# A state-space mixer times a spatial-shift MLP: new norms, polar form, layouts and a written-out instruction order

## The chip, the cores and the metric

The kernel runs on one core of one Trainium2 chip. Its time is the device time of one launch in microseconds, the median of several runs. A core has five engines that run side by side, each with its own queue in fixed order: TensorE (PE, matrix multiplication), VectorE (DVE, element-wise), ScalarE (ACT, table functions and copies), GpSimd (POOL, hardly used here) and SyncE (SP, which issues the DMAs). They wait for each other through semaphores.

## The reference

The input `u` is 2048 steps by 512 channels. It is normalised, and two branches work on the result; their product is added to the input.

```python
xn = _layernorm(x, axis=-1)
s = _A_ref(xn, A_re, A_im, B_re, B_im, C_re, C_im, log_dt, Dskip)
g = _silu(_B_ref(xn, w1, w2, w3, w4))
return x + s * g
```

Branch A is a long convolution. Its kernel `K[d, l]` is the real part of the sum over 128 states of `C * exp(dt * A * l) * dt * B`, complex; the convolution is done by FFT, and `xn * Dskip` is added. Branch B works along the steps and channels:

```python
h = _gelu(_layernorm(x) @ w1)
# the four quarters of h are shifted by +1, -1, +2, -2 steps
x1 = x + shifted(h) @ w2
return x1 + _gelu(_layernorm(x1) @ w3) @ w4
```

with `w1`, `w2` 512 x 512, `w3` 512 x 1376 and `w4` 1376 x 512.

## The kernel before

The 2048 steps are kept as 16 tiles of 128 partitions by 512 channels, one array `X`. Tile `s` holds the steps that are `s` modulo 16, with the four blocks of partitions in the order 0, 2, 1, 3 (`ORDER`). A shift by one or two steps is therefore mostly another tile; only at the two ends (tiles 0, 1 and 14, 15) does a shift also move by one partition. `wrapped` builds these shifted rows as copies into a tile `hw`.

The stages, by function:

- `loads` brings in X, the weights and the coefficients; `params` turns the coefficients into logarithm, angle, phase and magnitude for each channel and state. The phase and magnitude of `B * C` come from a polar form: the smaller over the larger of the two absolute values, an arctangent, and corrections for the swap and for both signs.
- `token_mixing` is branch B up to `x1`: `ln_first` normalises X (the first and the second norm in one step), `h_pair` transposes two tiles and multiplies by `w1` (f32, tile `pb`), `hs_pair` multiplies the shifted tiles by `w2` (f32, tile `pd`), `ln_second` prepares the norm for the MLP. `rstd` is an inverse square root by a guess and three Newton steps of three instructions on DVE. `u_stage1` makes the first stage of the FFT of u, stored in DRAM (`scr_Ud`); `weight_squares` and `prep` scale `w3` and `w4` and split them into f16 halves.
- `u_spectra` computes u's spectra of one half of the channels and stores them (`scr_Uh`).
- `tables(0)` and `tables(1)` compute the convolution kernel of one half of the channels each, in 8 tiles of 32 channels. `block` makes magnitudes (`mag`, `EB`) by exponentials on ACT; `phases`, `remainders`, `waves` and `sums` make sines and cosines and the products on DVE (`pt`), and two groups of 64 matmuls (`pc<-pt`) sum over the states.
- `kstage1` and `products` are the FFT stages: spectra, complex products, and the way back (`pr`, `z1e`), through DRAM.
- `mlp` multiplies by `w3` (`pb<-x1T,w3h`, 12 matmuls of one group, f16 in three passes), applies gelu and multiplies by `w4` (`pa<-w4h,ghl`, 6 matmuls of one group), for 8 groups of two tiles.
- `gate`, `inverse` and `finish` apply silu, multiply by the convolution's result and add the input.

None of this is issued in the order of the code. Each call is recorded as an operation of a `Plan`, with its cost in a model and its dependencies; a group in `together` is one operation. Operations of `E` (`Either`) can go to ACT or to DVE, the final stores to SP or ACT. `Plan.order` then schedules the list: whenever an engine is free it takes, of the ready operations, the one with the smallest due time (`DUE`, one number for each operation), with added prices for a change of ACT's table (`SWITCH`), of TensorE's mode (`KEEP`) and for the choice between ACT and DVE (`PREFER`, `AVOID` and their PSUM forms). `Plan.issue` emits the instructions in that order, with a table load wherever ACT's set changes and with warm-up matmuls (`fill`) where the model sees TensorE waiting. All instructions carry line 515 in the profile (512 for table loads, 514 for warm-up matmuls).

Of the kernel before, what the change touches and what calls it, by code (L numbers as in the profile page):

```python
# [10 lines left out]
F32 = mybir.dt.float32  # L11
# [8 lines left out]
P = 128  # L20
# [7 lines left out]
TWO_PI = 6.283185  # L28
INV_2PI = float(np.float32(1.0 / (2.0 * np.pi)))
# [63 lines left out]
class Op:  # L93
    __slots__ = (
        "eng", "alts", "calls", "cost", "deps", "succ", "table", "vt", "idx", "nbytes", "n", "ready", "start",
        "alias", "first", "last", "psum", "mode", "stage", "dma", "room", "fresh", "free_at", "fill",
# [23 lines left out]
SHIFT, KEEP = 0.09, 1.0  # L120
FETCH = 1.3, 5.0, 2.5
WORDS, ASKED, HELD, MORE = 256, 150, 449, 1.0065
WARM = 36
QUARTERS, EIGHTHS, SPECTRUM = 1.78, 1.8, 0.93
UP, DOWN = 1.31, 1.297

DUE = (
# [129 lines left out]
)  # L257
SWITCH = 20.74
PREFERP, AVOIDP = 12.42, -13.86
PREFER, AVOID = -0.38, -5.84  # L260

# [1266 lines left out]
```

## Time and profile before

| | |
|---|---|
| median of 3 runs | 562.91 us (561.33 to 565.46) |
| the profiled execution | 561.96 us, span in the profile 560.2 us |
| PE busy | 533.4 us, 95% |
| DVE busy | 466.1 us, 83% |
| ACT busy | 410.2 us, 73% |
| ACT table loads | 49, 62.9 us |
| DMA | 103.14 MB, 184 GB/s |

The span runs from the first to the last instruction of one execution. "Busy" of an engine counts the time in which at least one of its instructions runs; consecutive instructions overlap a little. Matmuls are pipelined, so PE's busy share is not its share of peak. Groups of instructions are listed as engine, operation, output tile <- input tiles, shapes and count, then busy time and mean duration in ns of one, then the engine's idle time before them with what ended it. The chain of work that ended last lists start, duration and what ran. The table of stretches lists for each engine the busy time and the number of instructions, then the granted TensorE clock, the DMA share and GB/s.

### The profile page before, as it was taken

To read this page: it belongs to the slowest core of one execution; us is meant where nothing else is said; L and a number is where in the kernel's file an instruction comes from. 1 tells how busy PE (TensorE), PEld (TensorE's weight loads), DVE (VectorE), ACT (ScalarE), POOL (GpSimd) and SP (SyncE) were. 2 spreads that over 40 slices of the span, in tenths; PEclk is the share of its full clock that TensorE was granted. 3 is DMA by queue.
4 is the path that set the end of the run, shared out by engine and by line. 5 is a ranking of instruction groups with operands and counts; after the bars stand their busy time and mean duration, and the time that the engine had idled before them with its cause. 6 is when DMAs were issued, how large, how long until landed. Compare 5 with 4: busy or idle time off the path is not lost.

```text
span 560.2 us, 14282 instructions
## 1 busy us (share of the span) xinstructions
PE 533.4 (95%) x6104; PEld 349.6 (62%) x6104; DVE 466.1 (83%) x710; ACT 410.2 (73%) x588; POOL 0.7 (0%) x6
## 2 busy tenths in 40 slices
PE   7989999989899899999999999999999999999982
PEld 7967677855344466656766666676676665675630
DVE  5999999999999998999999999999415168564276
ACT  2999997999987998998899999768246235224420
POOL 0000000000000000000000000000000000000000
PEclk9999999999999899999999999999999999999995
DMA  9975667535647252735333431453886669859947
GB/s 205 229 214 190 233 222 253 180 117 165 196 143 263 96 140 68 217 140 186 112 100 100 133 131 60 142 162 124 264 281 236 225 190 281 254 156 277 327 130 223
DMA packets 69695, 103.14 MB, mean 184 GB/s; under 512 B 14784, under 2 KB 48832, under 8 KB 68736
## 3 DMA queue, kind: packets, MB, share of 16 engines
q1 hardware_dynamic: 68864, 100.13, 57.8%
q10 hardware_dynamic: 768, 2.10, 1.2%
q8 instruction: 48, 0.79, 0.6%
q14 instruction: 15, 0.12, 0.1%
HBM read 64.46 MB, written 37.75 MB: 182 GB/s over the span
## 4 chain that ended last, share of the span: by engine, by line
PE 72%; DVE 15%; ACT 5%; DMA 5%; issue 2%; SPq 1%; DVEq 0%; ACTq 0%
PE pb L515 29%; PE pa L515 21%; PE pd L515 11%; PE pc L515 11%; DVE pt L515 9%; DVE X L515 3%; DMA X<-in_A_u_dram 2%; ACT mag L515 2%; DMA w<-in_B_w_dram 2%; ACT pt L515 1%; DVE w4h L515 1%; SPq L515 1%; ACT L512 1%; DVE w3h L515 1%; DMA out_dram<-X 0%
## 5 line engine op out<-in xcount | busy, mean ns | idle before, releaser
L515 PE MATMUL pb<-x1T,w3h 128*128 128x256 f16 (+1 forms) x1056 | 123.4, 273 | 2.7 <-issue 1.2
L515 PE MATMUL pa<-w4h,ghl 128*128 128x512 f16 (+1 forms) x528 | 121.7, 379 | 0.0
L515 PEld LDWEIGHTS <-w3h 128*128 128x128 f16 (+1 forms) x1056 | 102.6, 100 | 28.5 <-issue 13.9
L515 PEld LDWEIGHTS <-ghl 128*128 128x128 f16 (+1 forms) x528 | 49.9, 98 | 59.7 <-issue 7.5
L515 DVE SCALAR_TENSOR_TENSOR ghl<-g,wsc,ghl 128x512 f16<-128x512 f32 (+1 forms) x48 | 33.6, 700 | 41.7 <-ACT ghl L515 41.6
L512 ACT ACT_TABLE_LOAD x49 | 62.9, 1283 | 7.4 <-DMA out_dram<-X 5.8
L515 PE MATMUL pd<-w,hT 128*128 128x512 f32 x116 | 56.8, 633 | 5.3 <-DVE X L515 4.3
L515 PE MATMUL pb<-xT,w 128*128 128x256 f32 x256 | 59.6, 384 | 1.9 <-ACT hT L515 1.4
L515 ACT ACTIVATE pt<-pt 128x2048 f32<-128x2048 f32 x29 | 55.2, 1906 | 7.6 <-DVE pt L515 7.6
L515 DVE TENSOR_TENSOR pt<-mag,pt 128x1024 f32<-128x1024 f32 x48 | 57.5, 1214 | 0.0
L515 ACT ACTIVATE g<-pb,wsc 128x512 f32<-128x512 f32 (+1 forms) x48 | 30.8, 649 | 35.6 <-PE pb L515 33.8
L515 PEld LDWEIGHTS pb<-xT,w 128*128 128x128 f32 x256 | 47.1, 190 | 13.4 <-ACT hT L515 3.6
L515 ACT ACTIVATE ghl<-g,wsc 128x512 f16<-128x512 f32 (+1 forms) x41 | 28.0, 688 | 30.0 <-PE pa L515 29.7
L515 PEld LDWEIGHTS pd<-w,hT 128*128 128x128 f32 x116 | 22.4, 201 | 33.9 <-issue 26.1
L515 ACT ACTIVATE mag<-par 128x128 f32<-128x128 f32 x160 | 41.0, 452 | 0.2
L515 DVE TENSOR_TENSOR pt<-pt 128x2048 f32<-128x2048 f32 x16 | 36.5, 2280 | 0.0
L515 DVE SCALAR_TENSOR_TENSOR pt<-pt 128x2048 f32<-128x2048 f32 x16 | 36.4, 2277 | 0.0
L515 PEld LDWEIGHTS pc<-pt 128*32 128x32 f32 x2048 | 29.5, 110 | 7.9 <-issue 5.8
L515 PE MATMUL pc<-pt 128*32 128x64 f32 x2048 | 32.5, 220 | 0.0
L515 ACT ACTIVATE pt<-pt,halfpi 128x2048 f32<-128x2048 f32 x16 | 32.0, 1998 | 0.1
L515 DVE TENSOR_TENSOR pr<-pd,uin 128x1024 f32<-128x1024 f32 x16 | 18.9, 1218 | 10.9 <-PE pd L515 10.8
L515 ACT ACTIVATE pt<-pt,magic 128x2048 f32<-128x2048 f32 x12 | 24.0, 1996 | 4.6 <-DVE pt L515 4.6
(149 smaller groups left out, 773.8 us busy)
## 6 DMA issues: line engine op xcount, KB each, us to landing
wst<-in_B_w_dram SPq DMA_DIRECT2D x20, 512.0 KB, 4.2
scr_Ud<-ue SPq DMA_DIRECT2D x16, 512.0 KB, 3.2
uin<-scr_Ud SPq DMA_DIRECT2D x32, 256.0 KB, 4.3
cst<-c_gp SPq DMA_DIRECT2D x16, 384.0 KB, 3.7
scr_Uh<-uh SPq DMA_DIRECT2D x8, 512.0 KB, 3.6
scr_Kfa<-k1e SPq DMA_DIRECT2D x8, 512.0 KB, 2.6
kin<-scr_Kfa SPq DMA_DIRECT2D x16, 256.0 KB, 3.2
scr_Zda<-z1e SPq DMA_DIRECT2D x8, 512.0 KB, 4.7
```

The source lines that it names most:

```text
L512: self.engines["ACT"].preload_act_table_set(SETS[table])
L515: ins = [getattr(self.engines[op.eng], name)(*args, **kw).ins for name, args, kw in op.calls]
```

## The change

The instructions change in these places:

- `rstd`: two third-order steps of four instructions in place of three Newton steps of three.
- `params`: the polar form takes the ratio of difference and sum of the absolute values, so that no swap has to be undone; the two signs become factors of plus or minus one half. The phase is scaled when it is copied into `par`.
- `ln_first`: four groups of tiles (2, 2, 4, 8) in place of five; the chain of the first one is a single operation of the plan. `ln_second`: four groups in place of six.
- The shifted rows are written by the gelu itself (`gelus`), in pieces, for the first and last pair; `wrapped` and `hw` are gone.
- `u_spectra` writes the spectra back into the tile of their inputs; the ring of input tiles and that of constants move.
- `block`: the lower half of the magnitudes (`mag[0]`) and `EB` are laid out in whole rows of 128 channels, so that the exponentials write and the squares read them in one piece; DVE then reads them with a step of 512 bytes.
- `Plan.order` no longer chooses: `SEQUENCE` lists all 1660 operations in order, and `CHOICE` names the engine of each of the 284 operations that have two. The order of the DMAs is part of it.

```diff
-        while len(out) < len(ops):
-            t, e = min(
-                (max(free[e], min(o.ready for o in pool)), e) for e, pool in pools.items() if pool
-            )
...
+        for k in SEQUENCE:
+            pick = ops[k]
+            assert pick.n == 0
+            e = pick.eng
+            t = max(free[e], pick.ready)
...
-        for f in (1.0, 1.0, by):
-            V.scalar_tensor_tensor(t, dst, -0.5 * f, dst, op0=ALU.mult, op1=ALU.mult)
+        for f in (0.375, 0.375 * by):
+            c = f ** 0.5
+            V.scalar_tensor_tensor(t, dst, c, dst, op0=ALU.mult, op1=ALU.mult)
             V.tensor_mul(t, t, x)
-            V.scalar_tensor_tensor(dst, t, 1.5 * f, dst, op0=ALU.add, op1=ALU.mult)
+            V.scalar_tensor_tensor(t, t, -10.0 / 3.0 * c, t, op0=ALU.add, op1=ALU.mult)
+            V.scalar_tensor_tensor(dst, t, 5.0 * f, dst, op0=ALU.add, op1=ALU.mult)
...
-        V.tensor_tensor(swap, tb, ta, op=ALU.is_gt)
-        V.tensor_tensor(am, ta, tb, op=ALU.max)
-        V.tensor_tensor(rat, ta, tb, op=ALU.min)
+        V.tensor_add(am, ta, tb)
+        V.tensor_sub(rat, tb, ta)
...
-        V.tensor_mul(am, am, tb)
+        V.scalar_tensor_tensor(am, tb, SQRT_HALF, am, op0=ALU.mult, op1=ALU.mult)
         V.tensor_mul(am, am, dtb)
+        V.tensor_scalar(sx, wr, 0.0, 0.5, op0=ALU.is_ge, op1=ALU.subtract)
+        V.tensor_scalar(wi, wi, 0.0, 0.5, op0=ALU.is_ge, op1=ALU.subtract)
         A.activation(ph, rat, AF.Arctan)
-        V.tensor_scalar(ph, ph, INV_2PI, None, op0=ALU.mult)
-        V.tensor_scalar(ta, ph, -2.0, 0.25, op0=ALU.mult, op1=ALU.add)
-        V.tensor_mul(ta, ta, swap)
-        V.tensor_add(ph, ph, ta)
-        V.tensor_scalar(tb, wr, 0.0, None, op0=ALU.is_lt)
-        V.tensor_scalar(ta, ph, -2.0, 0.5, op0=ALU.mult, op1=ALU.add)
-        V.tensor_mul(ta, ta, tb)
-        V.tensor_add(ph, ph, ta)
-        V.tensor_scalar(tb, wi, 0.0, -2.0, op0=ALU.is_lt, op1=ALU.mult)
-        V.scalar_tensor_tensor(ph, tb, 1.0, ph, op0=ALU.add, op1=ALU.mult)
+        V.scalar_tensor_tensor(ph, ph, -QUARTER, sx, op0=ALU.add, op1=ALU.mult)
+        V.scalar_tensor_tensor(ph, ph, QUARTER, wi, op0=ALU.add, op1=ALU.mult)
...
-        mag = [at(magn + 4 * K4 * h, [P, 8, BQ, 4], F32, "mag") for h in range(2)]
-        ea = EB[:, : 8 * BQ].rearrange("p (q a) -> p q a", a=8)
-        eb = EB[:, 8 * BQ :].rearrange("p (q b) -> p q b", b=4)
+        rows_of = at(magn, [P, 8, 4, BQ], F32, "mag")
+        mag = [rows_of.rearrange("p b c q -> p b q c"), at(magn + 4 * K4, [P, 8, BQ, 4], F32, "mag")]
+        ea = EB[:, : 8 * BQ].rearrange("p (a q) -> p q a", a=8)
+        eb = EB[:, 8 * BQ :].rearrange("p (b q) -> p q b", b=4)
...
-            uh = usr["uh"]([P, 2, 2, DH], F32, "uh")
+            uh = uin.rearrange("p (l a) d -> p l a d", a=2)
...
+    UP_ROW = ((64, 0, 64), (32, 64, 32), (1, 96, 31)), 0
+    DOWN_ROW = ((0, 64, 64), (64, 32, 32), (96, 1, 31)), 127
+
+    def gelus(j, m2, dst, src):
+
+        if 0 < j < S // 2 - 1:
+            A.activation(dst, src, AF.Gelu_apprx_tanh)
+            return
+        k = 1 if j == 0 else 0
+        steps = slice(0, 2) if m2 else slice(1 - k, 2 - k)
+        A.activation(dst[:, 1 - k], src[:, 1 - k], AF.Gelu_apprx_tanh)
+        if not m2:
+            A.activation(dst[:, k, k], src[:, k, k], AF.Gelu_apprx_tanh)
+        pieces, zero = DOWN_ROW if k else UP_ROW
+        for d, o, n in pieces:
+            A.activation(dst[:, k, steps, d : d + n], src[:, k, steps, o : o + n], AF.Gelu_apprx_tanh)
+        V.memset(dst[:, k, steps, zero : zero + 1], 0.0)
...
-            if j in (0, 1, 2, 4, 6):
-                ln_first(slice(2 * j, 2 * j + (2 if j < 2 else 4)))
+            if j in (0, 1, 2, 4):
+                ln_first(slice(2 * j, 2 * j + (2, 2, 4, 0, 8)[j]))
...
-            if k in (0, 1, 6, 7):
+            if k in (0, 7):
                 ln_second(slice(2 * GROUPS[k], 2 * GROUPS[k] + 2))
-            elif k in (3, 5):
-                ln_second(slice(2 * GROUPS[k - 1], 2 * GROUPS[k - 1] + 4))
+            elif k == 2:
+                ln_second(slice(4, 8))
+            elif k == 6:
+                ln_second(slice(8, 16))
```

More of the change, by code (lines that the diff above doesn't have):

```diff
@@ L28 @@
 TWO_PI = 6.283185
+QUARTER = float(np.pi / 4)
+SQRT_HALF = float(np.sqrt(0.5))
 INV_2PI = float(np.float32(1.0 / (2.0 * np.pi)))
@@ L94 @@
     __slots__ = (
-        "eng", "alts", "calls", "cost", "deps", "succ", "table", "vt", "idx", "nbytes", "n", "ready", "start",
-        "alias", "first", "last", "psum", "mode", "stage", "dma", "room", "fresh", "free_at", "fill",
+        "eng", "alts", "calls", "cost", "deps", "succ", "table", "idx", "nbytes", "n", "ready", "start",
+        "alias", "first", "last", "mode", "dma", "room", "fresh", "free_at", "fill",
     )
@@ L119 @@
 ISSUE = 0.45
-SHIFT, KEEP = 0.09, 1.0
+SHIFT = 0.09
 FETCH = 1.3, 5.0, 2.5
@@ L123 @@
 WARM = 36
+CHAIN = 2.3
 QUARTERS, EIGHTHS, SPECTRUM = 1.78, 1.8, 0.93
 UP, DOWN = 1.31, 1.297
-DUE = (
[129 rows of a table removed]
-)
-SWITCH = 20.74
-PREFERP, AVOIDP = 12.42, -13.86
-PREFER, AVOID = -0.38, -5.84
+SEQUENCE = (
[83 rows of a table added]
+)
+CHOICE = (
+    "AAAAADDAAAAAAADADAAADADDADDADADDDADADDDDDDDDDADDADADDDAAADADDAAAAAAAAAAAAAAAAAAAAAAAAAAADDADDAAAADDA"
+    "AAADAAAAAAADAAAAADAAADDAADDDAADDDAAAAAAAAAAAAAAAAAAAAAAAAAAAAAAAADDADAADDAAAAADAAAAAAAAAAADDDDADAAAA"
+    "AAAAAAAADAADDADDAAADDAAADAADADAADAADDAADADADDAAAAAADSSSSSSSSSSSSASSAASSAASSSSASAAASS"
+)
 class Clock:
@@ L356, in new @@
         op = Op()
-        op.alts, op.table, op.dma, op.psum = {}, table, dma, False
+        op.alts, op.table, op.dma = {}, table, dma
         op.deps, op.alias, op.idx = set(), set(), len(self.ops)
-        op.vt = DUE[op.idx]
         op.room, op.fresh, op.mode = set(), True, 0
@@ L366, in add @@
         op = self.group or self.new(table, dma)
-        op.psum = "PSUM" in str(reads[0].space) if reads else False
         if "PE" in alts:
@@ L433, in order @@
                 ops[d].succ.append(op)
-        pools = {e: [] for e in self.engines}
         free = dict.fromkeys(self.engines, 0.0)
-        def release(op):
-            for e in op.alts:
-                pools[e].append(op)
+        choice = iter(CHOICE)
         for op in ops:
-            if op.n == 0:
-                release(op)
-        table, mode, chan, landed, clock, words, out = 0, 0, 0.0, [], Clock(), Fetch(), []
-        while len(out) < len(ops):
-            t, e = min(
-                (max(free[e], min(o.ready for o in pool)), e) for e, pool in pools.items() if pool
-            )
-            pick, score = None, None
-            for o in pools[e]:
-                if o.ready <= t + 0.02:
-                    v = o.vt
-                    if e == "ACT" and o.table and o.table != table:
-                        v += SWITCH
-                    if e == "PE" and o.mode != mode:
-                        v += KEEP
-                    if len(o.alts) > 1:
-                        on = (PREFERP, AVOIDP) if o.psum else (PREFER, AVOID)
-                        v += on[e != "DVE"]
-                    if pick is None or (v, o.idx) < score:
-                        pick, score = o, (v, o.idx)
-            for k in pick.alts:
-                pools[k].remove(pick)
-            pick.eng = e
+            if len(op.alts) > 1:
+                letter = next(choice)
+                op.eng = next(e for e in op.alts if e[0] == letter)
+            else:
+                op.eng = next(iter(op.alts))
+        table, mode, chan, landed, clock, words, out = 0, 0, 0.0, [], Clock(), Fetch(), []
+        for k in SEQUENCE:
[3 more added lines that the diff above has]
+            t = max(free[e], pick.ready)
             pick.cost, pick.calls = pick.alts[e]
@@ L500, in order @@
                     s.free_at = max(s.free_at, after)
-                if s.n == 0:
-                    release(s)
         self.span = max(max(free.values()), chan)
@@ L766 @@
     gtile = Ring(area(2 * K2), K2, 2)
-    hw = at(gtile.o, [P, 6, P], F32, "hw")
     late = place[0]
@@ L799 @@
     usr = dict(
-        uin=Slots([early + 4 * K4, vtile.o]), uh=Slots([vtile.o + K4, wtile.o]), cst=Ring(wtile.o + K4, K1, 2),
+        uin=Slots([early + 4 * K4, vtile.o + K4]), cst=Ring(gtile.o + K2, K1, 2),
     )
@@ L890, in params @@
         sr = at(phA + 2 * K4, [P, 2, 4, NM], F32, "sr")
-        swap, rat = sr[:, 0], sr[:, 1]
-        V.tensor_tensor(swap, tb, ta, op=ALU.is_gt)
-        V.tensor_tensor(am, ta, tb, op=ALU.max)
-        V.tensor_tensor(rat, ta, tb, op=ALU.min)
+        sx, rat = sr[:, 0], sr[:, 1]
+        V.tensor_add(am, ta, tb)
+        V.tensor_sub(rat, tb, ta)
         V.tensor_scalar(ta, am, 1e-37, None, op0=ALU.max)
@@ L918, in params @@
             for h in range(2):
-                E.copy(
-                    par[:, k, h * DH : h * DH + DH].rearrange("p (m r) -> p m r", r=4),
-                    pt[:, h * DH : h * DH + DH].rearrange("p (r m) -> p m r", r=4),
-                )
+                dst = par[:, k, h * DH : h * DH + DH].rearrange("p (m r) -> p m r", r=4)
+                src = pt[:, h * DH : h * DH + DH].rearrange("p (r m) -> p m r", r=4)
+                if k == 2:
+                    E.affine(dst, src, 2.0 / np.pi)
+                else:
+                    E.copy(dst, src)
     lgr, thr, phr, wmr = par[:, 0, :], par[:, 1, :], par[:, 2, :], par[:, 3, :]
@@ L960, in squares @@
             for h in range(2):
-                A.activation(
-                    mag[b // 4][:, 2 * b % 8 + h : 2 * b % 8 + 2 * n : 2, :, 0:4:2],
-                    mag[0][:, b : b + n, :, 2 * h : 2 * h + 2], AF.Square,
-                )
+                src = rows_of[:, b : b + n, 2 * h : 2 * h + 2]
+                if b == 4:
+                    dst, src = mag[1][:, h : 2 * n : 2, :, 0:4:2], src.rearrange("p b c q -> p b q c")
+                else:
+                    dst = rows_of[:, 2 * b + h : 2 * b + 2 * n : 2, 0:4:2]
+                A.activation(dst, src, AF.Square)
         with plan.together(table=TABLES[AF.Exp]):
@@ L1293, in ln_first, with norms @@
             V.bn_aggr(mv[:, s, 0:2], stats[:, s % 8])
-        var, t = mv[:, ss, 1], tn[:, ss, 0]
-        V.tensor_scalar(t, var, EPS, None, op0=ALU.add)
-        V.reciprocal(t, t)
-        V.tensor_mul(mv[:, ss, 2], var, t)
-        rstd(r12[:, ss], mv[:, ss, 1:3], xe[:, ss], tn[:, ss])
-        V.scalar_tensor_tensor(bs[:, ss], mv[:, ss, 0], -1.0, r12[:, ss, 0], op0=ALU.mult, op1=ALU.mult)
+        def norms():
+            var, t = mv[:, ss, 1], tn[:, ss, 0]
+            V.tensor_scalar(t, var, EPS, None, op0=ALU.add)
+            V.reciprocal(t, t)
+            V.tensor_mul(mv[:, ss, 2], var, t)
+            rstd(r12[:, ss], mv[:, ss, 1:3], xe[:, ss], tn[:, ss])
+            V.scalar_tensor_tensor(bs[:, ss], mv[:, ss, 0], -1.0, r12[:, ss, 0], op0=ALU.mult, op1=ALU.mult)
+        if ss.start:
+            norms()
+        else:
+            with plan.together(cost=CHAIN):
+                norms()
         for s in steps:
@@ L1326, in h_pair @@
                         )
-            A.activation(h[:, 2 * m2 : 2 * m2 + 2], ph, AF.Gelu_apprx_tanh)
+            gelus(j, m2, h[:, 2 * m2 : 2 * m2 + 2], ph)
     def u_stage1(s):
@@ L1340 @@
     SH = (-1, 1, -2, 2)
-    WRAPS = ((0, S - 1), (2, S - 2), (2, S - 1), (1, 0), (3, 0), (3, 1))
-    def wrapped(k):
-        m, s = WRAPS[k]
-        src, dst = hT[s // 2][:, m, s % 2], hw[:, k]
-        if m % 2 == 0:
-            V.tensor_copy(dst[:, 64:P], src[:, 0:64])
-            V.tensor_copy(dst[:, 32:64], src[:, 64:96])
-            V.tensor_copy(dst[:, 1:32], src[:, 96:127])
-            V.memset(dst[:, 0:1], 0.0)
-        else:
-            V.tensor_copy(dst[:, 0:64], src[:, 64:P])
-            V.tensor_copy(dst[:, 64:96], src[:, 32:64])
-            V.tensor_copy(dst[:, 96:127], src[:, 1:32])
-            V.memset(dst[:, 127:P], 0.0)
     def hs_pair(s0):
@@ L1364, in hs_pair @@
                 for m in range(4):
-                    t = s + SH[m]
-                    if 0 <= t < S:
-                        w = hT[t // 2][:, m, t % 2]
-                    else:
-                        w = hw[:, WRAPS.index((m, t % S))]
+                    t = (s + SH[m]) % S
+                    w = hT[t // 2][:, m, t % 2]
                     T.matmul(acc[i], w, w2s[m], start=m == 0, stop=m == 3)
@@ L1443, in token_mixing @@
         for j in range(8):
-            if j in (0, 1, 2, 4, 6):
-                ln_first(slice(2 * j, 2 * j + (2 if j < 2 else 4)))
+            if j in (0, 1, 2, 4):
+                ln_first(slice(2 * j, 2 * j + (2, 2, 4, 0, 8)[j]))
             h_pair(j)
             u_stage1(2 * j)
-            if j == 0:
-                for k in range(3, 6):
-                    wrapped(k)
-        for k in range(3):
-            wrapped(k)
         for i in range(12):
```

212 rows, old and new, of tables (DUE, SEQUENCE) are left out of this document.

## The prediction

> **What bounds the kernel now.** I read the busy time by stage first, then the chain of work that ended last, then the groups of instructions. The stretches below are cut at 206.5 us (the last tile of the token mixing has gone through TensorE), at 395.4 us (the last tile of the second `tables` leaves TensorE) and at 541.5 us (the last matmul of the MLPs).
>
> ```profile
> core 0: us, PE busy (x) PEld busy (x) DVE busy (x) ACT busy (x) POOL busy (x), PEclk, DMA share, GB/s
> 0.00:206.50 206.50, 194.72 (x2033) 131.86 (x2034) 196.48 (x355) 184.01 (x307) 0.70 (x6) 0.98 0.63 190
> 206.50:395.40 188.90, 187.38 (x2606) 124.50 (x2604) 185.89 (x256) 169.94 (x212) 0.00 (x0) 1.00 0.42 131
> 395.40:541.50 146.10, 144.91 (x1348) 91.57 (x1342) 70.18 (x85) 53.89 (x69) 0.00 (x0) 1.00 0.77 242
> 541.50:560.20 18.70, 6.34 (x129) 1.72 (x128) 13.50 (x15) 2.34 (x2) 0.00 (x0) 0.66 0.68 204
> ...
> 111.40:185.70 74.30, 67.54 (x868) 35.18 (x868) 74.13 (x92) 68.35 (x101) 0.00 (x0) 0.98 0.54 176
> 185.70:240.00 54.30, 52.78 (x544) 32.83 (x544) 52.09 (x99) 52.33 (x94) 0.00 (x0) 0.97 0.43 125
> ```
>
> Two engines are full at once. DVE works 382 of the first 395 us; TensorE works all of the next 146 us, where DVE idles half the time. Between 111 and 240 us TensorE has holes (6.8 and 1.5 us), because DVE is late with what it needs. So the end is: when DVE has the last table ready, plus the TensorE work that is still left then, plus a tail of 18.7 us. The start is a third limit:
>
> ```profile
> 19.07 9.65 DMA w<-in_B_w_dram
> 28.73 0.64 issue
> 29.37 1.28 ACT L512
> 30.66 2.12 ACT mag L515 x8
> 32.78 0.86 ACT xT L515
> 33.65 0.04 issue
> 33.69 2.00 PE pb L515 x8
> ...
> 2.00:28.73 26.73, 24.16 (x200) 23.59 (x200) 20.91 (x58) 15.97 (x46) 0.00 (x0) 1.00 1.06 238
> ```
>
> TensorE's first real matmul (`h_pair`, tile pb) starts at 33.69 us: `w1` lands at 28.7, and then 5.0 us go to a table load, eight exponentials and the copy of xT, all on ACT. Until then TensorE runs only warm-up matmuls. The queue brings 238 GB/s.
>
> **The change part by part.** Numbering the operations in the order in which the code creates them turns the fixed sequence into an order for each engine; the counts below are read from it.
>
> *Start.* `w1` now stands behind X rows 0 to 7 (2 MB), five coefficient arrays (1.25 MB) and one w3 tile (0.5 MB); with itself (1 MB) that is 4.75 MB of 2^20 bytes, 4.98e6 bytes, where 238 GB/s over 26.7 us brought 6.36e6 before. At 238 GB/s from 2 us it lands at 22.9 us. The copy of xT is ACT's sixth piece of work, ahead of all exponentials, so the first matmul can start near 23.7 us, 10.0 us earlier. The row of those exponentials stands with ACT below. In TensorE's order the transposes of X rows 2 and 3 stand ahead of it and need ACT behind 20 exponentials (20 by 0.255 us): about 22 us, just in time; each us late there delays the first matmul by as much. DVE does not lose by the swap: it begins with the norm of X rows 0 and 1, whose 0.5 MB land at about 4.3 us, in place of the coefficients. X rows 8 to 11 land near 28 us and 12 to 15 near 35, and stand in DVE's order behind some 27 and 35 us of work that begins at 5: no wait. `w2`, three more w3 and w4 tiles and the spectra's loads follow on SP's queue as before, between the stores of Ud; I cost that at nothing, covered by the 0.63 DMA share of this stretch.
>
> *DVE, before the last table.*
>
> ```profile
> L515 DVE TENSOR_TENSOR sr<-tm 128x512 f32<-128x512 f32 x2 | 1.3, 684 | 0.0
> L515 DVE TENSOR_SCALAR tm<-pn 128x512 f32<-128x512 f32 x3 | 1.2, 413 | 0.0
> L515 DVE COPY hw<-hT 128x64 f32<-128x64 f32 x6 | 1.0, 185 | 0.0
> L515 DVE SCALAR_TENSOR_TENSOR rs<-rs 128x8 f32<-128x8 f32 x18 | 2.7, 150 | 0.0
> ...
> 37.11 0.21 DVE L515 SCALAR_TENSOR_TENSOR rs<-rs 128x8 f32<-128x8 f32 x2
> ...
> L515 DVE TENSOR_SCALAR pt<-pt 128x2048 f32<-128x2048 f32 x4 | 4.9, 1217 | 0.0
> L515 DVE COPY z1e<-pd 128x1024 f32<-128x1024 f32 x3 | 3.6, 1215 | 0.0
> L515 DVE TENSOR_SCALAR ghl<-g,wsc 128x512 f16<-128x512 f32 x5 | 2.4, 480 | 2.1 <-ACT g L515 1.9
> ```
>
> Instructions that follow each other overlap: two of 0.15 us take 0.21, so one costs about 0.08 us less than its mean. The polar form goes from 19 instructions to 12: four fewer of 0.684 and three fewer of 0.413, spaced 4 by 0.60 and 3 by 0.33, so -3.4. The shifted rows lose 18 copies and 2 memsets: at 0.10 (spaced) -2.0, at 0.185 -3.3; I take -2.0. The norms go from 5 and 6 groups to 4 and 4, and each inverse root from 11 small steps to 10 (with the 4 or 1 around it, 75 + 72 = 147 small instructions become 56 + 44 = 100). At 0.07 that is -3.3, at 0.15 -7.0; I take 0.10, -4.7. Against this, the fixed choices give DVE more: three more shifts by `magic` and three more absolute values (1.14 spaced, +6.8), one more copy each of xT and ue (+2.3), and narrow ones such as ghl, x1n and x1T (+0.8); and fewer z1e, k1e and kev copies (3, 1 and 2, the last at 0.60: -5.8) and three weight halves less (about half of the 2048-wide row each, -1.7). Together +2.4. Sum -7.7, ends -6.3 and -11.3. DVE's queue is full here, so this is worth its face value as long as DVE waits no longer than now.
>
> *TensorE after the last table.* The total work is the same; what counts is how much is left.
>
> ```profile
> L515 PE MATMUL pa<-w4h,ghl 128*128 128x512 f16 x216 | 49.7, 380 | 0.0
> L515 PE MATMUL pb<-x1T,w3h 128*128 128x256 f16 x408 | 47.9, 273 | 1.2 <-issue 1.2
> ...
> L515 PE MATMUL pb<-x1T,w3h 128*96 128x256 f16 x48 | 6.0, 274 | 0.0
> ...
> L515 PE MATMUL pa<-w4h,ghl 96*128 96x512 f16 x24 | 5.8, 379 | 0.0
> ...
> 381.39 1.30 PE pa L515 x6
> 382.68 1.31 PE pb L515 x12
> ```
>
> After 395.4 us these are 456 matmuls of the first product (38 groups of 12, 1.31 us each) and 240 of the second (40 groups of 6, 1.30 us). In the new sequence 32 and 38 groups stand behind the last table: -7.9 and -2.6. One spectrum more (+1.0) and one set of transposes less (-0.5): -10.0. To have done 10 us more in 7.7 us less, TensorE must find 17.7 us: 10.0 come from the earlier start, the other 7.7 from the 8.3 us of holes between 111 and 240. That is nearly all of them, so I let 3.2 us of waits remain (ends -4, when DVE's own few waits go too, and +9, when none of the holes closes).
>
> *ACT* has 54 table loads instead of 49 and 14 more, shorter gelus, but hands six instructions of about 2.0 us to DVE, and 144 of 208 exponentials are written in whole rows.
>
> ```profile
> L515 ACT ACTIVATE pt<-pt,magic 128x2048 f32<-128x2048 f32 x12 | 24.0, 1996 | 4.6 <-DVE pt L515 4.6
> ...
> 196.34 4.08 ACT L515 ACTIVATE mag<-par 128x128 f32<-128x128 f32 x16
> ...
> 210.38 1.28 ACT L512 ACT_TABLE_LOAD   x1
> 211.67 0.69 ACT L515 ACTIVATE g<-pb,wsc 128x512 f32<-128x512 f32 x1
> ```
>
> Loads +6.4, gelus +3 at most (14 by the 0.2 that a narrow piece may take), shifts and absolutes -12: about 2.6 us less, more with the exponentials (now 0.255 each). ACT ends no sum; 184 of 206 us is its cover, and were that gone each us would come through. [...]
>
> U's spectra written back into their input tile make two slots serve where four did: a slot is free only when its store has landed. The order puts the eight spectra over some 90 us, so I cost it at nothing; if a store were late, the next spectrum would stand ahead of the MLP in TensorE's queue.
>
> *Tail.*
>
> ```profile
> 541.60 1.28 DVE L515 SCALAR_TENSOR_TENSOR X<-pa,wsc,X 128x1024 f32<-128x1024 f32 x1 [0.68 <-PE pa L515]
> ...
> 553.31 0.69 DVE L515 TENSOR_TENSOR X<-X,pc 128x512 f32<-128x512 f32 x1
> 554.03 1.23 DVE L515 TENSOR_TENSOR X<-X,xr 128x1024 f32<-128x1024 f32 x1
> ```
>
> After the last MLP matmul the new order has nine products and seven additions, where now there are eight and six: +0.6 and +1.2, so +1.8.
>
> *Sum*, against the profiled execution (561.96 us, of which the span is 560.2): -7.7 -10.0 +1.8 +3.2 = -12.7, so 549.3. The median of the three runs stands 0.9 above that execution, and I predict 550.
>
> **The rivals.** *The head start is lost.* If TensorE cannot be fed earlier, the 10.0 us of work stay behind the last table and only DVE's part and the tail count: 562.9 - 7.7 + 1.8 = 557. For it speaks that DVE is full from the start; against it, that the new order gives the first rows' norm to DVE before all coefficients.
>
> *Everything closes.* No wait remains and DVE's go too (end -4): 562.9 - 7.7 - 10.0 + 1.8 - 4 = 543.
>
> *The change does not do what it says.* Only the order within each queue reaches the chip. If the new order waits at its heads as long as it saves, the time stays at 562.
>
> *Whole rows are dear to read.* The new layout makes DVE read single floats 512 bytes apart, in two of the five `sums` and in `factors` of each of 16 tiles: 48 instructions. No DVE row shows such a read from SBUF.
>
> ```profile
> L515 ACT ACTIVATE wst<-wst 128x1024 f32<-128x1024 f32 x10 | 10.5, 1054 | 0.2 <-DMA wst<-in_B_w_dram 0.2
> L515 ACT ACTIVATE mag<-mag 128x1024 f32<-128x1024 f32 x8 | 9.2, 1156 | 0.0
> ...
> L515 DVE CAST x1T<-pb 128x512 f16<-128x512 f32 x3 | 2.0, 680 | 0.0
> L515 DVE COPY kev<-pc 128x512 f32<-128x512 f32 x3 | 2.0, 680 | 0.0
> ```
>
> On DVE a copy that reads PSUM 256 bytes apart (kev) takes as long as one in a row (x1T), so zero is the lower end, and I take it. On ACT a strided pass through SBUF takes 10% more, which on DVE would be 0.12 us each, 5.8 in all. If DVE read at two thirds of its speed, 0.4 us each, 19 us would be added where DVE is full: 569. It turns the gain into a loss from 0.27 us each. [...]
>
> **How the numbers follow.** Forecast 550: 0.55, own range 544 to 555. Everything closes: 0.11. Head start lost: 0.15. Nothing gained: 0.08. Dear rows: 0.11. The range 541 to 561 leaves out the dear rows and the edges. Within 1% (5.6 us, about what a measurement of this kernel can tell) lie the nothing-gained case and a sliver of the lost head start; so faster 0.80, same 0.09, slower 0.11.
>
> **What would show it.** Right: pb's first matmul at 23 to 25 us; the last 128 matmuls of pc<-pt near 388 to 391 us, with 32 and 38 groups behind them; `hw` gone; mag and EB readers on DVE still 1.21 us; table loads x54 of 1283 ns; a tail of some 20.5 us. Wrong: mag and EB readers at 1.3 us or more; TensorE's holes before 240 us as large as now; a long wait at the head of DVE's or ACT's queue that the old order did not have.

## The result, and the profile after

The changed kernel takes 593.63 us (median of 4 runs, 591.98 to 594.40) where the kernel before took 562.12 beside it: a ratio of 1.055, 95% interval 1.0512 to 1.0587. The prediction was 550, so it was wrong in sign. The profiled execution took 591.98 us, with a span of 590.2.

First the busy time by stage, cut at the prediction's second and third point: the last tile of the second `tables` leaves TensorE at 431.4 us (before: 395.4), the last MLP matmul ends at 565.8 (before: 541.5).

```profile
core 0: us, PE busy (x) PEld busy (x) DVE busy (x) ACT busy (x) POOL busy (x), PEclk, DMA share, GB/s
0.00:431.40 431.40, 395.81 (x4647) 264.74 (x4648) 419.72 (x533) 355.94 (x542) 0.70 (x6) 0.97 0.48 147
431.40:565.80 134.40, 134.40 (x1279) 82.99 (x1284) 70.25 (x94) 46.20 (x58) 0.00 (x0) 1.00 0.81 258
565.80:590.20 24.40, 6.37 (x144) 1.73 (x138) 15.03 (x17) 2.10 (x2) 0.00 (x0) 0.69 0.67 198
```

Beside the prediction's rows for the kernel before, the span grew by 30.0 us: 36.0 more to the last table, 11.7 less of TensorE's work behind it (134.4 for 146.1), 5.7 more tail (24.4 for 18.7). Ahead of the last table DVE executes 533 instructions where it had 611, and is busy 37.4 us longer (419.7 for 196.5 + 185.9). Which instructions, the groups of DVE show (count, then busy us and mean ns), first of the kernel after, then of the kernel before:

```profile
L453 DVE TENSOR_TENSOR pt<-mag,pt 128x1024 f32<-128x1024 f32 x48 | 82.4, 1727 | 0.2
L453 DVE TENSOR_TENSOR pt<-EB 128x1024 f32<-128x1024 f32 x16 | 33.4, 2088 | 0.0
L453 DVE SCALAR_TENSOR_TENSOR pt<-mag,pt 128x1024 f32<-128x1024 f32 x16 | 19.5, 1217 | 0.2
```

```profile
L515 DVE TENSOR_TENSOR pt<-mag,pt 128x1024 f32<-128x1024 f32 x48 | 57.5, 1214 | 0.0
L515 DVE TENSOR_TENSOR pt<-EB 128x1024 f32<-128x1024 f32 x16 | 19.3, 1213 | 0.0
```

Of the 48 products, 16 read the half of `mag` that kept its layout; with those at 1.21, the 32 that read whole rows take (82.4 - 16 x 1.21) / 32 = 1.97 us each. The 16 `factors`, which read EB, take 2.09. The third row, which reads the kept half, is unchanged. Together 24.9 + 14.1 us, and 1.5 more in four smaller products with EB: 40.5 us. This is what the prediction had at zero.

The chain of work that ended last now runs through DVE: 47% of the span (before 15%) with 31% in `pt` alone (before 9%). Its link to TensorE is the last table:

```profile
DVE 47%; PE 35%; ACT 9%; issue 4%; DMA 3%; SPq 1%; DVEq 0%; ACTq 0%
...
425.01 1.97 DVE pt L453
428.15 1.23 DVE pt L453
429.42 1.99 PE pc L453 x128
431.42 1.42 PE pb L453 x12
```

The start, on the timeline of TensorE and of ACT:

```profile
21.15 4.05 PE L452 MATMUL pd<-ident 128*128 128x128 f32 x30
25.04 0.60 PE L453 MATMUL pd<-ident,x 128*128 128x128 f32 x4
25.48 5.34 PE L453 MATMUL pb<-xT,w 128*128 128x256 f32 x24
```

```profile
23.62 0.71 ACT L453 ACTIVATE x<-X,rs 128x512 f32<-128x512 f32 x1
```

The first matmul of `h_pair` starts at 25.48, 8.2 us earlier than before. It stands behind the transposes of X rows 2 and 3 (`pd<-ident,x`), and those need ACT's scaled copy, which ends at 24.3. They start only at 25.0, since warm-up matmuls (line 452) still run ahead of them in TensorE's queue.

### The profile page after: what moved, and what is told of

Read it like the earlier page. It is cut to its first block, busy times and chain, and to the rows that moved or that the text cites. A ratio compares the mean times of both kernels' runs of the same rounds, so it can differ in the third digit from the quotient of the medians.

```text
span 590.2 us, 14127 instructions
## 1 busy us (share of the span) xinstructions
PE 536.6 (91%) x6058; PEld 349.5 (59%) x6058; DVE 505.0 (86%) x643; ACT 404.2 (68%) x601; POOL 0.7 (0%) x6
## 4 chain that ended last, share of the span: by engine, by line
DVE 47%; PE 35%; ACT 9%; issue 4%; DMA 3%; SPq 1%; DVEq 0%; ACTq 0%
DVE pt L453 31%; PE pb L453 13%; PE pa L453 11%; PE pc L453 7%; PE pd L453 5%; DVE pr L453 4%; DVE X L453 4%; ACT mag L453 3%; DVE ghl L453 2%; ACT pt L453 2%; DVE x1T L453 1%; DVE pab L453 1%; DMA rawC<-in_A_C_re_dram 1%; ACT L450 1%; DVE ue L453 1%
## 5 line engine op out<-in xcount | busy, mean ns | idle before, releaser
L453 PE MATMUL pb<-x1T,w3h 128*128 128x256 f16 (+1 forms) x1056 | 125.3, 274 | 0.8 <-DVE x1T L453 0.8
L453 PEld LDWEIGHTS <-w3h 128*128 128x128 f16 (+1 forms) x1056 | 103.4, 101 | 27.7 <-issue 11.1
L453 DVE TENSOR_TENSOR pt<-mag,pt 128x1024 f32<-128x1024 f32 x48 | 82.4, 1727 | 0.2
L450 ACT ACT_TABLE_LOAD x54 | 69.3, 1283 | 7.1 <-DVE X L453 6.2
L453 PE MATMUL pd<-w,hT 128*128 128x512 f32 x128 | 62.6, 640 | 7.5 <-DVE X L453 5.6
L453 ACT ACTIVATE pt<-pt 128x2048 f32<-128x2048 f32 x26 | 49.5, 1903 | 11.0 <-DVE pt L453 11.0
L453 PEld LDWEIGHTS pb<-xT,w 128*128 128x128 f32 x256 | 47.1, 190 | 12.2 <-issue 3.2
L453 PEld LDWEIGHTS pd<-w,hT 128*128 128x128 f32 x128 | 25.1, 203 | 37.8 <-issue 28.1
L453 PE MATMUL pc<-pt 128*32 128x64 f32 x2048 | 35.4, 229 | 11.2 <-DVE pt L453 11.1
L453 PEld LDWEIGHTS pc<-pt 128*32 128x32 f32 x2048 | 32.1, 116 | 19.7 <-DVE pt L453 14.4
L453 ACT ACTIVATE ghl<-g,wsc 128x512 f16<-128x512 f32 (+1 forms) x32 | 22.1, 699 | 25.9 <-PE pa L453 23.2
L453 ACT ACTIVATE mag<-par 128x128 f32<-128x128 f32 x160 | 36.9, 361 | 2.4 <-DVE pt L453 2.3
L453 DVE TENSOR_TENSOR pt<-EB 128x1024 f32<-128x1024 f32 x16 | 33.4, 2088 | 0.0
```

Source lines behind the costliest of these rows:

```text
L450: self.engines["ACT"].preload_act_table_set(SETS[table])
L453: ins = [getattr(self.engines[op.eng], name)(*args, **kw).ins for name, args, kw in op.calls]
```

## The experiments

All are edits of the changed kernel, but for one that edits the kernel before. Where the old layout of `mag` is put back, a few operations of `block` on ACT change places among themselves, because its squares and exponentials then depend on each other.

**The layouts: both, each, and alone.** One kernel puts both layouts back, two put back one each:

```
-        rows_of = at(magn, [P, 8, 4, BQ], F32, "mag")
-        mag = [rows_of.rearrange("p b c q -> p b q c"), at(magn + 4 * K4, [P, 8, BQ, 4], F32, "mag")]
-        ea = EB[:, : 8 * BQ].rearrange("p (a q) -> p q a", a=8)
-        eb = EB[:, 8 * BQ :].rearrange("p (b q) -> p q b", b=4)
+        mag = [at(magn + 4 * K4 * h, [P, 8, BQ, 4], F32, "mag") for h in range(2)]
+        ea = EB[:, : 8 * BQ].rearrange("p (q a) -> p q a", a=8)
+        eb = EB[:, 8 * BQ :].rearrange("p (q b) -> p q b", b=4)
```

Both:

> The changed kernel with both layouts of before: EB and mag hold their four (or eight) values of one q side by side again. Everything else of the change stays: sequence, polar form, norms, shifted rows, start. Theory (DVE pays for the strided reads): after the change the 32 products with the whole-row half of mag take 1.98 us instead of 1.21, the 16 factors 2.09 instead of 1.21, four small products 1.04 instead of 0.68: 24.6 + 14.1 + 1.5 = 40 us of DVE, and DVE has no idle time before the last table. Then these rows fall back to about 1.21, DVE's busy time from 505 to about 465, and the time to 550 to 557. Rival (the new order costs too: the three table loads ahead of the h pair, gelu pieces ahead of the sines): rows fall as said, but the time stays above 572, since other waits take over. Rival that the reads are not the cause: rows stay near 2 us.

EB alone (the last two lines):

> The changed kernel with EB as before, mag in whole rows. Theory (the strided reads set the pace, each at its face value): 14.1 + 1.5 us of DVE go and 24.6 stay, so 593.6 - 15.6 = 578, within 4. If only one of the two layouts mattered, and it were mag, it would stay at 590 or above.

`mag` alone (the second line):

> The changed kernel with mag as before, EB in whole rows. Theory (strided reads at face value): 24.6 us of DVE go and 15.6 stay, so 593.6 - 24.6 = 569, within 4. If the products with mag were covered by ACT's or TensorE's waits, it would stay above 580.

The fourth goes the other way: the kernel before with these lines of the change and nothing else, each queue held in its old order.

> The kernel before with one part of the change alone: EB and the first half of mag in whole rows, everything else, and each queue's order, as before. Theory (the strided reads cost their face value wherever DVE is full, whatever the order): about 40 us more work on DVE and 33 to 38 us more time, 595 to 600, with DVE's rows at 2.0 and 2.1 us. Rival (the dear reads hurt only together with the new order, or ACT's cheaper exponentials, 0.16 us less for each of 192, pay part of it back): under 585.

Measured: both back, 559.39 (0.996 of before, 0.9941 to 0.9979); EB back, 577.55 (1.0308, 1.0276 to 1.0340); `mag` back, 569.63 (1.0161, 1.0136 to 1.0186); whole rows alone in the kernel before, 596.73 (1.0617, 1.0599 to 1.0636). DVE's rows of the kernel with both back, then of the one with whole rows alone:

```profile
L461 DVE TENSOR_TENSOR pt<-mag,pt 128x1024 f32<-128x1024 f32 x48 | 57.9, 1216 | 0.2
L461 DVE TENSOR_TENSOR pt<-EB 128x1024 f32<-128x1024 f32 x16 | 19.5, 1216 | 0.0
```

```profile
L706 DVE TENSOR_TENSOR pt<-mag,pt 128x1024 f32<-128x1024 f32 x48 | 82.2, 1732 | 0.0
L706 DVE TENSOR_TENSOR pt<-EB 128x1024 f32<-128x1024 f32 x16 | 33.7, 2115 | 0.0
```

The layout's cost is shown from both sides: 34.2 us when it is taken out of the new kernel, 34.7 when it is put into the old one. Each part counts at its face value: EB's 15.4 us of DVE gave 16.1, `mag`'s 24.5 gave 24.0. Both together give 34.2 and not 40, since DVE then waits more: 16.9 us idle ahead of the last table (398.2 less 381.3, a row shown further below), where it had 11.7.

**What a strided read costs.** One kernel measures it by itself, behind its end, in a single execution. Another keeps 8-byte pairs in `mag`, and makes each product of two halves of 512 elements.

```
+    views = [flat[1], flat[2], flat[3], flat[4], flat[8], rows, quads[:, :], pair4, pair8, wide]
+    for k, src in enumerate(views):
+        V.tensor_mul(shaped(outs[k % 4], src)[:, : src.shape[1]], src, shaped(J, src)[:, : src.shape[1]])
...
+        for k in range(8):
+            V.tensor_mul(J[:, :n], J[:, :n], J[:, :n])
+        for k in range(8):
+            V.tensor_mul(outs[k % 4][:, n * k : n * k + n], R[:, :n], R[:, n : 2 * n])
```

> The kernel with both layouts of before, with DVE instructions added behind its end (time not compared): 1024-element products that read one operand at steps of 4, 8, 12, 16 and 32 bytes, in the whole-row pattern (single floats 512 bytes apart), in runs of four floats (16 bytes) every 128, in pairs every 16 and every 32 bytes, in fours 32 bytes apart; one with both operands strided, a copy, and two that write strided; then chains of 8-element products. [...] By a rule that any step costs: 2 us from 8 bytes on. By a rule of distance: more at 512 bytes than at 16. For the chains: 0.2 us for each product that needs the one just before it, under 0.1 for independent ones and for those put between wide ones.

The timeline of DVE, ten products of 1024 f32 in the order of `views`: steps of 4, 8, 12, 16 and 32 bytes, whole rows, four floats in a row every 128 bytes, pairs every 16 and every 32 bytes, and fours at 32-byte steps. Then a copy from whole rows and a copy in a row, a product written in whole rows, and two chains of eight 8-element products: each needs the one before, then independent.

```profile
562.26 1.16 DVE L461 TENSOR_TENSOR O<-R,J 128x1024 f32<-128x1024 f32 x1
563.34 1.21 DVE L461 TENSOR_TENSOR O<-R,J 128x1024 f32<-128x1024 f32 x1
564.47 1.50 DVE L461 TENSOR_TENSOR O<-R,J 128x1024 f32<-128x1024 f32 x1
565.89 1.96 DVE L461 TENSOR_TENSOR O<-R,J 128x1024 f32<-128x1024 f32 x1
567.77 1.98 DVE L461 TENSOR_TENSOR O<-R,J 128x1024 f32<-128x1024 f32 x1
569.66 1.90 DVE L461 TENSOR_TENSOR O<-R,J 128x1024 f32<-128x1024 f32 x1
571.48 1.21 DVE L461 TENSOR_TENSOR O<-R,J 128x1024 f32<-128x1024 f32 x1
572.61 1.21 DVE L461 TENSOR_TENSOR O<-R,J 128x1024 f32<-128x1024 f32 x1
573.75 1.21 DVE L461 TENSOR_TENSOR O<-R,J 128x1024 f32<-128x1024 f32 x1
574.88 1.98 DVE L461 TENSOR_TENSOR O<-R,J 128x1024 f32<-128x1024 f32 x1
...
578.73 1.15 DVE L461 COPY O<-R 128x1024 f32<-128x1024 f32 x1
579.80 0.67 DVE L461 COPY O<-R 128x1024 f32<-128x1024 f32 x1
580.40 1.89 DVE L461 TENSOR_TENSOR R<-J 128x1024 f32<-128x1024 f32 x1
...
586.15 1.57 DVE L461 TENSOR_TENSOR J<-J 128x8 f32<-128x8 f32 x8
587.63 0.70 DVE L461 TENSOR_TENSOR O<-R 128x8 f32<-128x8 f32 x8
```

In these rows the step from one float to the next sets the time, up to a point: 8 bytes cost next to nothing (1.21 for 1.16 in a row), 12 bytes 0.29 more than 8 (1.50), 16 bytes 0.75 more (1.96), and 32 bytes and whole rows no more than that (1.98 and 1.90). Single floats 16 bytes and more apart are dear, neighbours are not: pairs and fours take 1.21, with 16, 32 or 128 bytes from one group to the next, while the fours at 32-byte steps, of which no two are neighbours, take 1.98. The rule of distance is out (1.90 at 512 bytes, 1.96 at 16), and so is the rule that any step costs (1.21 at 8).

> EB as before; the whole-row half of mag is instead held in pairs of two neighbouring floats (8 bytes), the two pairs of one q 1024 bytes... apart by half a row set, and each of the 32 products with it is made in two instructions of 512 elements (one for each pair), since one instruction has too few dimensions. [...] By a fixed price for any layout that is not the old one: each half takes 1.04 us and the two 2.1, and the time is that of EB alone put back, about 578, or a little more. [...]

Measured: 558.71 (0.9951, 0.9926 to 0.9976), and 687 ns for each of the 64 halves, where 512 elements in a row take 680: no penalty is left, the fixed price of 1.04 us is out, and the halves agree with the probe's rows for pairs. It is 0.7 us below the kernel with both layouts back, less than the two intervals can tell apart.

**The tail.** With both layouts back the kernel still misses the forecast by 9. Its tail has DVE's last addition at 548.4 but ends at 557.6. `CHOICE` also decides which queue issues each of the 32 final stores, and it gives 23 to SP. One row is the timeline of SP in the kernel with both layouts back; then its stores, and those of the kernel that shares them out evenly, by queue (with their number, ns of each, first and last start):

```profile
548.49 6.53 SPq L461 DMA_DIRECT2D out_dram<-X  x13
```

```profile
L461 SPq DMA_DIRECT2D out_dram<-X x23: 314/420/882, 532.6 to 554.6; - x23
L461 ACTq DMA_DIRECT2D out_dram<-X x9: 321/383/434, 532.6 to 548.9; - x9
```

```profile
L461 ACTq DMA_DIRECT2D out_dram<-X x16: 321/376/1079, 531.7 to 548.5; - x16
L461 SPq DMA_DIRECT2D out_dram<-X x16: 314/403/1084, 536.1 to 549.9; - x16
```

```
-    "...AAAAAADSSSSSSSSSSSSASSAASSAASSSSASAAASS"
+    "...AAAAAADSASASASASASASASASASASASASASASASA"
```

> The kernel with both layouts of before (559.4 us), and the 32 stores of the output divided evenly over the two issuing queues (SP and ACT by turns) instead of 23 on SP and 9 on ACT. Theory (SP issues one store per 0.43 us, and 13 of them still stand behind the last addition at 548.4, so the last is issued at 554.6; before, where two of each four stood on either queue, the last was issued 0.4 us after the last addition): the last store is issued some 5 us earlier and the span ends 4 to 5 us earlier, 555. Rival (the stores are limited by the DMA engines' bandwidth, 2 MB still to be written): within 1 us of 559.4.

Measured: 555.15 (0.9883, 0.9848 to 0.9918). The last store is issued at 549.9 and not 554.6, and the time falls by 4.2. Bandwidth did not limit it: the tail moved 210 GB/s at a DMA share of 0.70 with 23 stores on SP, and moves 243 at 0.82 with even stores.

**What the head start is worth.** Two kernels load `w1` later in SP's queue, the first by 2 MB, the second (with even stores) by 4 MB:

```
-    ... 93, 27, 26, 9, 319, 115, 10, ...
+    ... 93, 27, 26, 30, 29, 28, 31, 11, 9, 319, 115, 10, ...
```

> The kernel with both layouts of before (559.4 us), and w1's two halves moved in SP's queue behind X rows 8 to 11 and the first-stage constants, 2 MB: 8 us later, about where they landed before the change. Theory of the prediction (each us of earlier start of TensorE is worth its face value): first matmul of the h pair near 33 us, 7 to 8 us more in time, 567. Rival (DVE sets the last table, and TensorE's holes before 220 us take up the later start): at most 3 us more, 560 to 562.

> The kernel with both layouts of before and even stores (555.2 us), and w1's halves behind all X rows and the constants, 4 MB later in SP's queue. The 2 MB tried before delayed the first h pair little (first matmul still at 26.1, then 3.2 us of waits for w1); at 240 GB/s these 4 MB put w1 some 17 us later, near 37 us, 11 to 12 us behind the 25.9 of now. Theory of the prediction (an earlier start is worth its face value): 11 us more, 566. Rival (TensorE has holes before 220 us that take up part of it, and the last table is DVE's): 2 to 6 us more, 557 to 561.

TensorE's timeline in the second, and in the kernel with even stores that it starts from:

```profile
29.96 2.07 PE L461 MATMUL pb<-xT,w 128*128 128x256 f32 x4 [3.77 <-DMA w<-in_B_w_dram]
32.86 7.46 PE L461 MATMUL pb<-xT,w 128*128 128x256 f32 x20 [0.82 <-DMA w<-in_B_w_dram]
```

```profile
25.91 5.35 PE L461 MATMUL pb<-xT,w 128*128 128x256 f32 x24
```

Here the 24th matmul ends 9.1 us later (40.3, not 31.3). The last table comes 9.3 later (407.3, not 398.0), and the time is 8.8 more: 563.98 (1.0035, 1.0022 to 1.0048) for 555.15. DVE loses it too: between 20 and 60 us it is busy 31.0 us where it was 39.3. The first kernel was a weaker probe than meant, since its first matmul stayed at 26.1 and only the later ones came 1.8 late. Its last table comes 1.8 later (400.0, not 398.2), and it took 561.17 (0.9975, 0.9960 to 0.9991), 1.8 more than without, but only 0.8 by the ratios, whose intervals overlap. So the second kernel carries the proof: in this sequence a us by which TensorE starts later costs a us. The rival, that holes swallow it, falls. A start earlier still was not tried.

**The norms' small steps.**

```
+            if ops[k].eng == "DVE" and prev in ops[k].deps and dict(ops[k].alts)["DVE"][0] < 0.3:
+                ...  # take one of the next wide DVE operations that is ready first
```

> The same as the kernel with even stores, and in DVE's order no small step of an inverse root stands directly behind the one it needs, where a wide instruction that is ready can be put between. Theory (41 of 132 small steps come 0.2 us after the one before them, where a step between two wide instructions adds 0.075): some 20 of the 41 can be woven, 20 by 0.12 = 2.5 us less on DVE, and 2 to 3 us less in time. Rival (the norm comes later by the wide instructions now in between, and TensorE waits for it): the same or up to 4 us more.

Measured: 557.53 (0.9914, 0.9884 to 0.9944), 2.4 more than with even stores alone, with intervals that overlap. Only 11 of the 41 steps could be woven. DVE's work ahead of the last table fell by 1.0 us, and its idle time rose by 3.9, so that this table came 2.9 later (400.9, not 398.0). The theory fails. The rival fits, but that it is the norm that is waited for is not shown.

**Six shifts back to ACT.**

```
     # CHOICE: ph shift 0, 1, 3, 5 and 13 and abs 11
-    D D D D D D
+    A A A A A A
```

> The kernel with both layouts of before and even stores (555.2 us), and six of the 13 magic shifts and absolute values that DVE does given to ACT, as many as before the change. DVE loses 6 by 1.15 = 6.9 us ahead of the last table, ACT gains 6 by 2.0 = 12. Theory (DVE alone sets the last table): it comes up to 6.9 us earlier, 548 to 551. Rival (ACT, at 186 of 206 us and 173 of 192, is nearly as full, and DVE waits for what ACT does later): the last table moves by less than 2 us, or later; 554 to 560.

Both theories missed: 584.51 (1.0390, 1.0366 to 1.0414). DVE's work ahead of the last table fell by 5.7 us as expected, but that table came at 427.4 for 398.0. Two rows of its waits (us in all, times, longest), and its busy time up to that table:

```profile
DVE pt L461 <- ACT pt L461: 19.0, 8, 6.2
ACT pt L461 <- DVE pt L461: 11.0, 4, 6.6
```

```profile
0.00:427.40 427.40, 399.93 (x4705) 270.17 (x4706) 375.73 (x527) 369.55 (x548) 0.70 (x6) 0.97 0.48 149
```

DVE now idles 51.7 us there, where it idled 16.6. It waits eight times for ACT in `pt`, 19.0 us in all, where the kernel with even stores has 1.5; three of these waits, 15.2 us, stand at the instruction that reads a shift. ACT waits four times for DVE. The likely reason is that the sequence places these operations for DVE, but no run shows it, and how the 29 us come about in detail I leave open.

**Pairs and even stores together.** Both edits shown above.

> Pairs (8 bytes side by side in mag's first half, each product in two instructions) and even stores together, EB as before. Each alone: pairs 0.7 us less than the old layout, even stores 4.2 less. If they add: 554.5, about 1.3% below the kernel before; the last store near 549.7 and the last table near 398. If pairs' smaller ACT time counts more once the stores are gone: 553.

Measured: 555.97 (0.9891, 0.9870 to 0.9912). The pairs add nothing that can be told from the 555.15 of even stores alone. Both versions beat the kernel before by 1.1 to 1.2%.

## Why the prediction was wrong, step by step

The sum had -4.5 to the last table (DVE -7.7, waits that remain +3.2), -10.0 of work behind it and +1.8 of tail. The kernel with both old layouts shows the rest of the change without the strided reads:

```profile
0.00:398.20 398.20, 386.18 (x4653) 261.55 (x4654) 381.34 (x533) 359.10 (x542) 0.70 (x6) 0.99 0.51 160
398.20:533.20 135.00, 134.92 (x1276) 83.00 (x1284) 70.23 (x93) 46.12 (x58) 0.00 (x0) 1.00 0.79 253
533.20:557.60 24.40, 6.82 (x144) 1.79 (x144) 15.05 (x17) 2.16 (x2) 0.00 (x0) 0.65 0.70 210
```

Against before it stands at +2.8, -11.1 and +5.7, and the strided reads add 33.2 to the last table.

- **Strided reads, at zero: the step that failed.** Measured +0.76 and +0.87 us for each 1024 elements, three times the 0.27 at which the prediction saw the gain turn into a loss; 34 us in time. The choice between the bounds was wrong, and so was the upper one (0.4): the row taken for zero reads PSUM, and the other is ACT's. Neither showed DVE's reads from SBUF. ACT's row was no test of single floats either: its squares read two neighbours of every four floats and write every second one, and for reads in these two patterns the probe has 1.21 us on DVE, where a row takes 1.16. The rival's price was also reckoned too low: two thirds of the speed (measured: 0.61 for `mag`, 0.58 for EB) is 0.6 us more on 1.21, which gives 29 us and 579, not 0.4 and 569. What the prediction named as a sign of its error, readers at 1.3 us or more, is what the profile shows. Dear rows were named as a rival and given a chance of only 0.11.
- **Norms, -4.7: measured near nothing.** By how far each step moves DVE's end it is +0.4; it lies between -0.1 and +1.1 as the short gaps inside a chain are counted as idle or as work. The count was right (147 small steps became 100, besides 32 aggregates each). Before, they stood one by one between wide instructions and added 0.075 each. Now 41 follow the step that they need:

```profile
7.06 0.17 DVE L461 TENSOR_SCALAR rs<-mv 128x4 f32<-128x4 f32 x1
7.26 0.17 DVE L461 TENSOR_SCALAR rs<-rs 128x4 int32<-128x4 int32 x1
7.47 0.16 DVE L461 SCALAR_TENSOR_TENSOR rs<-rs 128x4 f32<-128x4 f32 x1
```

```profile
15.58 0.16 DVE L515 RECIPROCAL rs<-rs 128x2 f32<-128x2 f32 x1
15.65 0.41 DVE L515 TENSOR_SCALAR tm<-pn 128x512 f32<-128x512 f32 x1
15.97 0.15 DVE L515 TENSOR_TENSOR mv<-mv,rs 128x2 f32<-128x2 f32 x1
```

  The first fence is the kernel with both old layouts: a step each 0.20 us, as in the chain of eight above (1.57 in all). The second is the kernel before: the wide one begins 0.07 behind the small one. The -4.7 charged 0.10 for each step wherever it stood. In the probe's second chain, where no product needs the one before, each costs 0.08 (eight in 0.70, the last of them 0.16 long).
- **The rest of DVE's sum held.** Counted by how far each instruction moves DVE's end, polar form -3.7 (predicted -3.4), shifted rows -1.7 (-2.0), choices +2.7 (+2.4). The wide rows left over gained 1.6 in sum, which I do not explain. So DVE's work fell by 1 us at most, not 7.7, and its idle time rose by 3.9 (16.9 for 13.0). That is why the last table did not come earlier even without the strided reads. TensorE shows the same from its side. The prediction let nearly all of its 8.3 us of holes between 111 and 240 close, and 7.1 remain (74.3 less 68.98, and 54.3 less 52.51), with DVE about as full there as before (73.6 and 52.9 us busy, for 74.1 and 52.1):

```profile
111.40:185.70 74.30, 68.98 (x883) 37.70 (x883) 73.63 (x85) 69.15 (x107) 0.00 (x0) 0.98 0.50 163
185.70:240.00 54.30, 52.51 (x599) 32.08 (x601) 52.90 (x83) 53.95 (x95) 0.00 (x0) 1.00 0.49 146
```

  From its first matmul of `h_pair` to the last table TensorE works 364.4 us where it worked 353.4. It starts 7.7 earlier (26.0) and idles 0.5 less, and so ends 2.8 later.
- **TensorE's work behind the last table, -10.0: right**, -11.1 measured, with 32 and 38 groups there as counted. The groups missing there stand ahead of the last table, where only the earlier start made room for them.
- **The start.** The first matmul came 8.2 earlier and not 10.0, for the reason that the prediction named, the transposes of X rows 2 and 3, and for one that it did not: ACT's copy for them ends at 24.3 and not 22, and warm-up matmuls hold them 0.7 more. With EB alone put back no warm-up stands in the way, and they start 0.05 behind the copy (24.08). That a us of a later start costs a us is shown.
- **Tail, +1.8: measured +5.7.** The DVE instructions were counted right. The queue of the final stores was not read, though `CHOICE` shows it; it cost 4.2.
- **ACT** has its 54 table loads of 1283 ns. With both old layouts it is busy 2.8 us less than before (407.4 for 410.2; predicted 2.6, without the exponentials). The narrow gelu pieces, estimated at 0.2 us, take 0.24 to 0.31 in the changed kernel, and the slots of u's spectra cost nothing that the chain shows.

## What to carry to other kernels

A layout is paid for by who reads it: before it is turned for the writer's sake, the readers' innermost step must be looked up, and two neighbouring f32 at a time were enough here to keep DVE's reads near the time of a row (1.21 us for 1.16). Where an operation's price is unknown and the engine is full, the nearest row must be of the same engine and the same memory, or the upper end must carry weight. In a fixed order count the small things by where they stand: a dependent step behind its source cost 0.2 us here and one between wide instructions 0.075, and the queue of each final store belongs to the tail.

## What the runs showed of the hardware that was not expected

- In the probe DVE's f32 product of 1024 elements takes 1.16 us in a row, 1.21 at 8-byte steps and in pairs or fours of neighbours, 1.50 at 12-byte steps, and 1.90 to 1.98 at steps of 16, 32 and 512 bytes. A product written in whole rows takes about as long (1.89). A copy of 1024 takes 1.15 from whole rows, for 0.67 in a row.
- ACT gains little by whole rows: an exponential of 128 elements into EB took 295 ns for 450, but such exponentials overlap, and the 48 of them kept ACT busy 10.0 us for 12.2. DVE loses 14 to read them.
- The 13 stores that SP's queue still held after the last addition took 6.5 us, 0.50 each on average.
